# Clustered attention with a Fourier and feed-forward layer: the first sequence's products with the values go three ticks behind the scores, six buffers of transposed probabilities, and the maxima of the later sequences written in place in PSUM

## Chip, cores and metric

The kernel runs on one core of a Trainium2 chip. The metric is the device time of one execution in microseconds (us). Five engines work side by side, each through its own instructions in order: PE (matmuls, with PEld for the loads of stationary operands), DVE (vector), ACT (scalar functions), POOL (a second, slower vector engine) and SP, which here only issues DMAs.

## What is computed

Four sequences of 768 tokens, 8 heads of 64. Queries and keys are each put into one of 16 clusters per head, and a query attends only to keys of its own cluster. The result goes through a two-dimensional Fourier transform with a residual, a layer norm and a feed-forward block.

```
q_assign = argmax(einsum('bhsd,hcd->bhsc', q_n, c_n), axis=-1)      # k_assign likewise
mask = q_assign[:, :, :, None] == k_assign[:, :, None, :]
scores = where(mask, scale * matmul(q, k.T), -1e9)
scores = scores - max(scores, axis=-1, keepdims=True)
attn = exp(scores); attn = attn / (sum(attn, axis=-1, keepdims=True) + 1e-09)
x = matmul(attn, v)                                                # (B, S, H*D)
u = x + real(fft(fft(x, axis=1), axis=2))
un = (u - mean(u)) / sqrt(var(u) + 1e-06)
out = u + relu(un @ w_ch1) @ w_ch2
```

All matmuls are made of fp16 pairs (a high and a low half), so that they come near fp32.

## The kernel before

Heads are worked in pairs: `pr` runs from 0 to 15, four pairs to a sequence. A pair has six tile rows of 128 queries (`st`). In what follows a *tile row* n of the first sequence is 6·pr + st, from 0 to 23. `Overlap.run` writes the whole program out over a clock of its own, in *ticks*: it puts every piece of work into a list under a tick and an order within the tick. In each tick stand, by that order: the scores of one tile row (`att.scores`, order 1), the product with the values of an earlier tile row (`att.attend`, order 3, LAG = 2 ticks after its scores), steps of the next pair's preparation (`att.prep`, `split_v`), and in the first 28 ticks a piece of the weights' preparation (order 6). PE follows this list exactly; on DVE, ACT, POOL and SP the order is made by a scheduler that places instructions when their inputs are due.

A tile row goes through the engines like this, once for each of its two heads (j = 0, 1):

- PE makes the scores in PSUM (L320 and L325, `ps_big`, two buffers).
- DVE takes the row maximum (L339): it multiplies the scores by a negative scale, writes the product somewhere, and keeps the minimum in `rmx`. In the first sequence (`early`) the product goes into one of four strips of X[1] in SBUF and is used; in the later ones it goes into a bf16 tile `ju` that nobody reads.
- ACT takes the exponential (L343 in the first sequence, from the strip; L345 later, from the scores in PSUM) and rounds it to fp16 (L353).
- POOL subtracts that from the exponential to get the low half (L354).
- SP issues one DMA that transposes both halves into a `pt` tile (L356). There are PT = 5 of these.
- In `attend`, PE multiplies `pt` with the values (L374, L375, L376, 36 matmuls to a tile row) into `ps_o`, which has one buffer and takes three tile rows.
- After every third tile row `finish` runs on DVE: L386 and L388 make the reciprocal of the sums, L390 scales `ps_o` into X and so frees it for the next three.

The values come as fp16 pairs in `v16` tiles, four buffers, two of them for one head pair: the split for pair pr + 2 (L199 on ACT, L200 on POOL, L201 on DVE) takes the buffers of pair pr, and so waits for that pair's last `attend`. The weights go through DVE, ACT, POOL and PE too: loaded by SP (L484) into eight raw buffers, their largest taken (L491), split into signs (L519, L520), joined by PE in PSUM (L528), completed by DVE (L532, which frees the raw buffer), and halved (L538, L541, L542, L544).

After a sequence's last tile row `fold` (L660, L661, L641, L642) starts the Fourier work, and from then on each sequence's Fourier and feed-forward matmuls (L713 and others, L858 up, L888 down) fill PE between the next sequence's scores.

Of the kernel before, what the change touches and what calls it, by code (L numbers as in the profile page):

```python
# [15 lines left out]
BF16 = mybir.dt.bfloat16  # L16
# [4 lines left out]
AF = mybir.ActivationFunctionType  # L21
# [4 lines left out]
P = 128  # L26
# [5 lines left out]
SH = S // 2  # L32
# [49 lines left out]
class Attention:  # L82
# [226 lines left out]
    def scores(self, pr, st):  # L309
        nc, sb = self.nc, self.sb  # L310
        assert self.ready >= pr
        (hq, hk), oh, (e, ne) = self.hl[pr], self.oht[pr], self.sc.scores(pr)
        sl = slice(st * P, (st + 1) * P)
        ps = [self.psum().rearrange("p (h x) -> p h x", h=2) for _ in range(2)]
        rows = [slice(D * j, D * (j + 1)) for j in range(2)]
        for hf in range(2):
            hs = slice(hf * SH, (hf + 1) * SH)
            for i, (a, c) in enumerate(((0, 0), (1, 0), (0, 1))):
                for j in range(2):
                    nc.tensor.matmul(out=ps[j][:, hf, 0:SH], lhsT=hq[rows[j], a, sl], rhs=hk[rows[j], c, hs],  # L320
                                     start=(i == 0), stop=False)
        for hf in range(2):
            for j in range(2):
                rz = slice(D * j + 32 * hf, D * j + 32 * hf + 32)
                nc.tensor.matmul(out=ps[j][:, hf, 0:SH].rearrange("p (s x) -> p s x", x=P), lhsT=oh[rz, st % 3 * 2 + st // 3],  # L325
                                 rhs=oh[rz, ST:], start=False, stop=True)
        for j in range(2):

            m = sb.tile([P, 1], F32, name="rmx", tag="rmx", bufs=6)
            early = pr < H // 2  # L330
            if early:

                n = (2 * st + j) % self.RING * S
                p32 = self.X[1].rearrange("p a x -> p (a x)")[:, n:n + S]
            else:
                p32 = sb.tile([P, S], F32, name="p32", tag="p32", bufs=2)
            x = p32.rearrange("p (h x) -> p h x", h=2)
            ju = x if early else sb.tile([P, 2, SH], BF16, name="ju", tag="ju")
            self.mark = nc.vector.tensor_scalar(out=ju, in0=ps[j][:, :, 0:SH], scalar1=ne, scalar2=None, op0=ALU.mult, op1=ALU.min,  # L339
                                    accum_out=m)  # L340
            self.late = m
            if early:
                nc.scalar.activation(p32, p32, AF.Exp, bias=m, scale=-1.0)  # L343
            else:
                nc.scalar.activation(x, ps[j][:, :, 0:SH], AF.Exp, bias=m, scale=e)  # L345
            if early and j:
                ph = sb.tile([P, S], F32, name="p32", tag="p32", bufs=2).bitcast(F16).rearrange("p (a x) -> p a x", a=2)
            else:
                ph = sb.tile([P, 2, S], F16, name="ph", tag="ph", bufs=2)
            if early and j and (st in self.PC):  # L350
                nc.gpsimd.tensor_copy(out=ph[:, 0], in_=p32)
            else:
                nc.scalar.copy(out=ph[:, 0], in_=p32)  # L353
            nc.gpsimd.tensor_tensor(out=ph[:, 1], in0=p32, in1=ph[:, 0], op=ALU.subtract)  # L354
            pt = sb.tile([P, 2 * ST, P], F16, name="pt", tag="pt", bufs=PT)
            nc.sync.dma_start(out=pt, in_=ph.rearrange("p a x -> p (a x)"), transpose=True)  # L356
            self.pt[pr, st, j] = pt
        if st == ST - 1:
            self.hl.pop(pr)
            self.oht.pop(pr)  # L360
# [534 lines left out]
            yield 2.6  # L895


PT = 5


class Overlap:
# [20 lines left out]
    MIX = (1, 0, 0, 0, 1, 0, 0, 1, 1, 0)  # L922
    MIX3 = (0, 0, 0, 0, 0, 0, 0, 1, 1, 1)
    F2 = 1
    PIN, PF, PV = (), 29, 1
    CE, WP, WQ = 0.45, 0, 0

    def layer(self, b, old):
# [52 lines left out]
    def run(self):  # L981
        att, T0, NP = self.att, self.T0, B * H // 2
# [3 lines left out]
        def at(t, order, f, *a):  # L986
            sched.setdefault(max(t, 0), []).append((order, len(sched.get(t, ())), f, a))
# [37 lines left out]
        for pr in range(NP):  # L1025
            t0 = T0 + 6 * pr
            for i, (t, order) in enumerate(self.STEPS if pr else self.STEPS0):
                at(t0 + t, order, (pinned if i in self.PIN and t0 + t >= self.PF else step) if pr else first, att.prep, pr)
            for st in range(ST):
                at(t0 + st, 1, att.scores, pr, st)  # L1030
                at(t0 + st + self.LAG, 3, att.attend, pr, st)
            a, d, e = self.V if pr else self.V0
            at(t0 + a, 7 if pr else 0.1, att.load_v, pr)
            at(t0 + d, 4.5, pin if self.PV and t0 + d >= self.PF else call, att.split_v, 2 * pr)
            at(t0 + e, 4.5, pin if self.PV and t0 + e >= self.PF else call, att.split_v, 2 * pr + 1)
# [81 lines left out]
```

## Time and profile before

| | |
|---|---|
| median of 3 runs | 1053.56 us (1049.64 to 1055.57) |
| the profiled execution | 1049.91 us, its span 1048.1 us |
| PE, DVE, ACT, POOL busy | 87%, 60%, 60%, 56% of the span |

The span is what the trace covers; some 1.8 us lie around it. The shares of busy time are means over stages with different limits: in roughly the first 210 us attention of the first sequence and the weights' preparation run together, later PE's feed-forward work sets the pace. So a stretch of its own has to be read for each.

### The profile page before, as it was taken

How to read it: one execution, taken by the hardware profiler on the slowest of the kernel's cores; microseconds unless marked ns; L12 is line 12 of the kernel's file. 1: busy time of each engine (PE TensorE's matmuls, PEld its weight loads, DVE VectorE, ACT ScalarE, POOL GpSimd, SP SyncE). 2: the span in 40 equal slices, each digit the busy share in tenths (PEclk: the TensorE clock that was granted, in tenths of full speed). 3: DMA queues.
4: the chain of work that ended last, by engine and by line, in shares of the span. 5: the costliest groups of instructions: out<-in, count | busy, mean ns of one | idle time of the engine just before them, and what ended most of it. 6: DMA issues, size and time to landing. Idle time of an engine off the chain costs nothing.

```text
span 1048.1 us, 23542 instructions
## 1 busy us (share of the span) xinstructions
PE 910.8 (87%) x9350; PEld 591.7 (56%) x9362; DVE 627.4 (60%) x1297; ACT 625.3 (60%) x980; POOL 586.9 (56%) x693
## 2 busy tenths in 40 slices
PE   3665565749899999998899999997999999999998
PEld 2333333425575756655666757555757667576674
DVE  8789899767757555668656555667555333631110
ACT  4798889755766665645666746556756543351230
POOL 2364565753975756655856646647847645271230
PEclk9987878769899999999899999998999999999999
DMA  7799998979887776568877767588757562321000
GB/s 272 179 225 245 196 239 166 171 156 153 177 123 153 128 154 121 121 137 161 153 137 142 140 128 132 110 141 170 124 102 133 96 110 43 81 52 31 11 11 21
DMA packets 396239, 140.01 MB, mean 134 GB/s; under 512 B 381784, under 2 KB 381792, under 8 KB 396128
## 3 DMA queue, kind: packets, MB, share of 16 engines
q1 hardware_dynamic: 396128, 138.50, 65.9%
q8 instruction: 73, 1.20, 0.5%
q14 instruction: 38, 0.31, 0.1%
HBM read 42.52 MB, written 6.29 MB: 47 GB/s over the span
## 4 chain that ended last, share of the span: by engine, by line
PE 39%; DVE 6%; DMA 3%; ACT 3%; POOL 2%; issue 2%; SPq 0%; ACTq 0%; DVEq 0%; POOLq 0%
PE ps_f L888 16%; PE ps_f L858 13%; PE ps_big L320 3%; DMA pt<-ph 3%; PE ps_f L713 2%; DVE ju L339 1%; ACT p L345 1%; PE ps_o L374 1%; POOL ph L354 1%; PE ps_o L375 1%; PE ps_o L376 1%; PE ps_big L325 1%; ACT ph L353 1%; DMA scr<-in_k_dram 0%; DVE arena L660 0%
## 5 line engine op out<-in xcount | busy, mean ns | idle before, releaser
L354 POOL TENSOR_TENSOR ph<-p,ph 128x768 f16<-128x768 f32 x144 | 242.9, 1688 | 184.6 <-ACT ph L353 150.1
L858 PE MATMUL ps_f<-arena,w1h 128*128 128x256 f16 x1536 | 271.4, 277 | 19.1 <-ACT arena L866 9.0
L888 PE MATMUL ps_f<-w2h,arena 128*128 128x512 f16 x768 | 238.9, 379 | 0.0
L345 ACT ACTIVATE p<-ps_big,rmx,sce 128x768 f32<-128x768 f32 x144 | 142.1, 988 | 132.9 <-DVE ju L339 127.5
L858 PE MATMUL ps_f<-arena,w1l 128*128 128x256 f16 x768 | 212.4, 277 | 0.0
L339 DVE TENSOR_SCALAR_CACHE_REDUCE ju<-ps_big,sce 128x768 bf16<-128x768 f32 x144 | 146.1, 1014 | 68.2 <-PE ps_big L325 58.2
L888 PEld LDWEIGHTS <-arena 128*128 128x128 f16 x1152 | 108.7, 98 | 126.6 <-issue 5.2
L858 PEld LDWEIGHTS <-w1h 128*128 128x128 f16 x1536 | 152.1, 99 | 36.0 <-issue 14.3
L867 POOL TENSOR_TENSOR arena<-arena 128x256 f16<-128x256 f32 x192 | 128.1, 677 | 77.3 <-ACT arena L866 73.6
L320 PE MATMUL ps_big<-hlk,hlq 64*128 64x384 f16 x1152 | 128.9, 348 | 39.0 <-ACT p L345 23.4
L374 PE MATMUL ps_o<-v,pt 128*128 128x66 f16 x1152 | 124.8, 198 | 43.0 <-DVE X L390 27.5
L888 PE MATMUL ps_f<-w2l,arena 128*128 128x512 f16 x384 | 145.5, 379 | 0.0
L374 PEld LDWEIGHTS <-pt 128*128 128x128 f16 x1152 | 110.2, 100 | 57.7 <-issue 37.1
L353 ACT CAST ph<-p 128x768 f16<-128x768 f32 x144 | 119.6, 832 | 15.0 <-DMA pt<-ph 12.8
L375 PE MATMUL ps_o<-v,pt 128*128 128x64 f16 x1152 | 124.8, 199 | 0.0
L376 PE MATMUL ps_o<-v,pt 128*128 128x66 f16 x1152 | 124.5, 198 | 0.0
L866 ACT ACTIVATE arena<-ps_f,wrel 128x256 f16<-128x256 f32 x192 | 90.1, 472 | 54.8 <-DVE arena L863 54.7
L863 DVE TENSOR_SCALAR arena<-ps_f,wrel 128x256 f32<-128x256 f32 x96 | 46.3, 482 | 124.9 <-PE ps_f L858 66.4
L320 PEld LDWEIGHTS <-hlq 64*128 64x128 f16 x1152 | 55.5, 99 | 101.5 <-issue 72.7
L375 PEld LDWEIGHTS <-pt 128*128 128x128 f16 x1152 | 110.7, 101 | 2.8
L376 PEld LDWEIGHTS <-pt 128*128 128x128 f16 x1152 | 111.1, 103 | 0.0
L858 PEld LDWEIGHTS <-w1l 128*128 128x128 f16 x768 | 76.1, 99 | 20.2 <-issue 10.7
(178 smaller groups left out, 1330.4 us busy)
## 6 DMA issues: line engine op xcount, KB each, us to landing
arena<-in_moe_w_ch_dram SPq DMA_DIRECT2D x32, 512.0 KB, 6.8
scr<-in_q_dram SPq DMA_DIRECT2D x16, 384.0 KB, 2.9
scr<-in_k_dram SPq DMA_DIRECT2D x16, 384.0 KB, 4.5
vst<-in_v_dram SPq DMA_DIRECT2D x16, 384.0 KB, 3.5
out_dram<-arena SPq DMA_DIRECT2D x24, 256.0 KB, 2.3
pt<-ph SPq DMA_TRANSPOSE x168, 3.9
arena<-in_cs_dram SPq DMA_DIRECT2D x12, 192.0 KB, 3.5
arena<-in_ss_dram SPq DMA_DIRECT2D x12, 192.0 KB, 3.5
```

The lines of the kernel that those rows point to most:

```text
L320: nc.tensor.matmul(out=ps[j][:, hf, 0:SH], lhsT=hq[rows[j], a, sl], rhs=hk[rows[j], c, hs], start=(i == 0), stop=False)
L339: self.mark = nc.vector.tensor_scalar(out=ju, in0=ps[j][:, :, 0:SH], scalar1=ne, scalar2=None, op0=ALU.mult, op1=ALU.min, accum_out=m)
L345: nc.scalar.activation(x, ps[j][:, :, 0:SH], AF.Exp, bias=m, scale=e)
L353: nc.scalar.copy(out=ph[:, 0], in_=p32)
L354: nc.gpsimd.tensor_tensor(out=ph[:, 1], in0=p32, in1=ph[:, 0], op=ALU.subtract)
L374: nc.tensor.matmul(out=o[:, at:at + W], lhsT=hi, rhs=v16[:, kt, 0:W], start=(kt == 0), stop=False)
L375: nc.tensor.matmul(out=o[:, at:at + D], lhsT=hi, rhs=v16[:, kt, 66:130], start=False, stop=False)
L376: nc.tensor.matmul(out=o[:, at:at + W], lhsT=lo, rhs=v16[:, kt, 0:W], start=False, stop=(kt == ST - 1))
L858: nc.tensor.matmul(out=ps.rearrange("p (t x) -> p t x", x=P), lhsT=a[:, dc, fs], rhs=c[:, :, dc], start=(i == 0), stop=(i == 11))
L866: nc.scalar.activation(hh[:, f], ps, AF.Relu, scale=rel[:, f:f + 1])
L867: nc.gpsimd.tensor_tensor(out=hl[:, f], in0=r, in1=hh[:, f], op=ALU.subtract)
L888: nc.tensor.matmul(out=ps, lhsT=a[:, f, ts], rhs=c[:, f], start=(i == 0), stop=(i == 47))
```

## The change

Three things. `attend` of tile rows 0 to 21 of the first sequence stands three ticks behind its scores in place of two; rows 22 and 23 stay at two, so that tile rows 21 and 22 are both multiplied in one tick, and the fold comes in the tick where it was. The `pt` tiles are six in place of five. In the later sequences the scaled, negated scores are written over the scores in PSUM, and the exponential reads them there with the scale −1, as it already does from SBUF in the first sequence; the `ju` tile is gone.

```
-        (hq, hk), oh, (e, ne) = self.hl[pr], self.oht[pr], self.sc.scores(pr)
+        (hq, hk), oh, ne = self.hl[pr], self.oht[pr], self.sc.scores(pr)[1]
...
-            ju = x if early else sb.tile([P, 2, SH], BF16, name="ju", tag="ju")
+            ju = x if early else ps[j][:, :, 0:SH]
             self.mark = nc.vector.tensor_scalar(out=ju, in0=ps[j][:, :, 0:SH], scalar1=ne, scalar2=None, op0=ALU.mult, op1=ALU.min,
                                     accum_out=m)
             self.late = m
-            if early:
-                nc.scalar.activation(p32, p32, AF.Exp, bias=m, scale=-1.0)
-            else:
-                nc.scalar.activation(x, ps[j][:, :, 0:SH], AF.Exp, bias=m, scale=e)
+            nc.scalar.activation(x, ju, AF.Exp, bias=m, scale=-1.0)
...
-PT = 5
+PT = 6
...
-    PIN, PF, PV = (), 29, 1
+    PIN, PF, PV, LATE = (), 29, 1, 22
...
-                at(t0 + st + self.LAG, 3, att.attend, pr, st)
+                at(t0 + st + self.LAG + (6 * pr + st < self.LATE), 3, att.attend, pr, st)
```

The numbers of lines below 338 are the same in both kernels; from the exponential on, a line of the kernel before has a number higher by 3 than in the changed one (L390 is L387 there).

**First place: PE, around the scores of tile row 22.** L325 ends the scores (`ps_big`); what follows is an `attend`. `pt_2218` is the transposed first head of tile row 20 in the kernel before.

```order
L325 MATMUL ps_big_2388<-oht_1914 128x384
L325 LDWEIGHTS oht_1914
L325 MATMUL ps_big_2389<-oht_1914 128x384
L374 LDWEIGHTS pt_2218
L374 MATMUL ps_o_2243<-v16_1684,pt_2218 128x66
```

In the changed kernel `pt_2097` is that of tile row 19.

```order
L325 MATMUL ps_big_2352<-oht_1874 128x384
L325 LDWEIGHTS oht_1874
L325 MATMUL ps_big_2353<-oht_1874 128x384
L371 LDWEIGHTS pt_2097
L371 MATMUL ps_o_2308<-v16_1647,pt_2097 128x66
```

So at the same place of PE's queue stands the product of a tile row that is one tick older.

**Second place: DVE, at the end of tile row 17, the sixth `finish`.** The pair of L339 on top is tile row 19 before, and the two single L339 are tile row 20.

```order
253 L339 TENSOR_SCALAR X_64,rmx<-ps_big,sce 128x768 x2
254 L216 TENSOR_REDUCE amx<-scr 128x1
255 L386 TENSOR_SCALAR rs<-ps_o,scp 128x6
256 L532 SCALAR_TENSOR_TENSOR ps_f<-arena,ps_f 128x512
257 L216 TENSOR_REDUCE amx<-scr 128x1
258 L388 RECIPROCAL rs<-rs 128x6
259 L544 SCALAR_TENSOR_TENSOR w2l<-ps_f,wsc,w2h 128x512
260 L201 SCALAR_TENSOR_TENSOR v_2280<-vst,scp,v_2280 128x6x64
261 L339 TENSOR_SCALAR X_64,rmx<-ps_big,sce 128x768
262 L390 TENSOR_TENSOR X_63<-ps_o,rs 128x3x128
```

In the changed kernel the same `finish` (L383, L385, L387) stands with tile row 20, whose two L339 are rows 262 and 266.

```order
259 L216 TENSOR_REDUCE amx<-scr 128x1 x2
260 L541 SCALAR_TENSOR_TENSOR w2l<-ps_f,wsc,w2h 128x512
261 L248 TENSOR_REDUCE amx<-vst 128x1
262 L339 TENSOR_SCALAR X_64,rmx<-ps_big,sce 128x768
263 L383 TENSOR_SCALAR rs<-ps_o,scp 128x6
264 L529 SCALAR_TENSOR_TENSOR ps_f<-arena,ps_f 128x512
265 L385 RECIPROCAL rs<-rs 128x6
266 L339 TENSOR_SCALAR X_64,rmx<-ps_big,sce 128x768
267 L387 TENSOR_TENSOR X_63<-ps_o,rs 128x3x128
```

Before, the freeing L390 stood behind the first maximum of tile row 20, and the next `attend` on PE came right after the scores of that row. Now L387 stands behind the second maximum of row 20, and the next `attend` comes only after the scores of row 21.

**Third place: DVE, at the fold of the first sequence.** L660, L661 and L642 are the fold and its halving; the L339 between them are tile rows of the second sequence.

```order
298 L660 TENSOR_TENSOR arena<-X_63 128x1536
299 L248 TENSOR_REDUCE amx<-vst 128x1
300 L642 SCALAR_TENSOR_TENSOR arena<-arena,vseq 128x768
301 L339 TENSOR_SCALAR ju,rmx<-ps_big,sce 128x768
302 L660 TENSOR_TENSOR arena<-X_63 128x1536
303 L339 TENSOR_SCALAR ju,rmx<-ps_big,sce 128x768
304 L201 SCALAR_TENSOR_TENSOR v_2839<-vst,scp,v_2839 128x6x64
305 L661 TENSOR_TENSOR arena<-arena 128x3x255
306 L642 SCALAR_TENSOR_TENSOR arena<-arena,vseq 128x768
```

The changed kernel has there:

```order
302 L657 TENSOR_TENSOR arena<-X_63 128x1536
303 L248 TENSOR_REDUCE amx<-vst 128x1
304 L339 TENSOR_SCALAR ps_big,rmx<-ps_big,sce 128x2x384 x2
305 L201 SCALAR_TENSOR_TENSOR v_2833<-vst,scp,v_2833 128x6x64
306 L639 SCALAR_TENSOR_TENSOR arena<-arena,vseq 128x768
307 L657 TENSOR_TENSOR arena<-X_63 128x1536
308 L658 TENSOR_TENSOR arena<-arena 128x3x255
309 L639 SCALAR_TENSOR_TENSOR arena<-arena,vseq 128x768
```

Both maxima now stand ahead of the first halving (L639), and nothing of the attention stands between it and the second.

## Rows read from the trace of the kernel before

**Rows 1.** Windows: width, busy us (instructions) by engine, clock, DMA share, GB/s.

```profile
56.00:208.50 152.50, 95.08 (x1176) 58.07 (x1187) 131.56 (x270) 132.61 (x190) 93.34 (x81) 0.80 0.98 207
208.50:262.00 53.50, 37.29 (x429) 22.82 (x431) 39.43 (x72) 29.01 (x43) 25.36 (x21) 0.81 0.85 156
262.00:1048.00 786.00, 749.47 (x7556) 496.54 (x7550) 411.84 (x844) 427.44 (x697) 450.46 (x546) 0.98 0.59 111
```

**Rows 2.** Waits of PE, 56 to 210 us: total us, times, longest.

```profile
PE ps_o L374 <- DVE X L390: 27.5, 6, 5.5
PE ps_o L374 <- DMA pt<-p: 7.4, 7, 2.6
PE ps_o L374 <- DMA pt<-ph: 6.8, 4, 2.2
```

**Rows 3.** Waits of DVE, 56 to 210 us.

```profile
DVE arena L491 <- DMA arena<-in_moe_w_ch_dram: 6.4, 5, 2.0
DVE ps_f L532 <- PE ps_f L528: 3.2, 3, 2.4
DVE ps_f L227 <- PE ps_f L48: 2.1, 2, 2.0
DVE X L339 <- PE ps_big L325: 1.1, 2, 0.6
```

**Rows 4.** Timeline of PE, 176 to 189.5 us: start, length, what, idle before.

```profile
178.49 0.34 PE L325 MATMUL ps_big<-oht 32*128 32x384 bf16 x4
...
183.71 0.19 PE L374 MATMUL ps_o<-v,pt 128*128 128x66 f16 x1 [4.28 <-DVE X L390]
...
187.13 0.24 PE L374 MATMUL ps_o<-v,pt 128*128 128x66 f16 x1 [2.61 <-DMA pt<-p]
...
188.51 1.49 PE L528 MATMUL ps_f<-arena 128*128 128x512 bf16 x3 [0.22 <-issue]
```

**Rows 5.** Timeline of DVE, 180 to 207 us.

```profile
183.01 0.55 DVE L390 TENSOR_TENSOR X<-ps_o,rs 128x384 f32<-128x384 f32 x1
...
189.18 0.70 DVE L532 SCALAR_TENSOR_TENSOR ps_f<-arena,ps_f 128x512 uint32<-128x512 uint32 x1 [2.39 <-PE ps_f L528]
...
206.22 0.57 DVE L227 TENSOR_REDUCE ps_f<-ps_f 128x3 f32<-128x384 f32 x1 [1.95 <-PE ps_f L48]
```

**Rows 6.** Windows, instructions that touch `ps_o`: width, PE and DVE busy us (instructions).

```profile
56.00:208.50 152.50, 34.70 (x723) 5.35 (x14) 0.80 0.98 207
```

**Rows 7.** Windows, instructions of L263: width, PE and PEld busy us (instructions).

```profile
56.00:208.50 152.50, 2.49 (x36) 0.86 (x36) 0.80 0.98 207
```

**Rows 8.** Timeline of DVE at the fold, 218.5 to 238.5 us.

```profile
227.35 1.41 DVE L642 SCALAR_TENSOR_TENSOR arena<-arena,vseq 128x768 f16<-128x768 f32 x1 [3.23 <-ACT arena L641]
228.69 1.00 DVE L339 TENSOR_SCALAR_CACHE_REDUCE ju<-ps_big,sce 128x768 bf16<-128x768 f32 x1
...
235.64 1.31 DVE L642 SCALAR_TENSOR_TENSOR arena<-arena,vseq 128x768 f16<-128x768 f32 x1 [1.00 <-ACT arena L641]
```

**Rows 9.** Groups on DVE by form, 56 to 210 us: busy us, mean ns, idle before.

```profile
L339 DVE TENSOR_SCALAR_CACHE_REDUCE X<-ps_big,sce 128x768 f32<-128x768 f32 x40 | 39.1, 1010 | 1.6 <-PE ps_big L325 1.1 <-POOL ac L281 0.5
L532 DVE SCALAR_TENSOR_TENSOR ps_f<-arena,ps_f 128x512 uint32<-128x512 uint32 x27 | 18.2, 688 | 3.3 <-PE ps_f L528 3.2
L60 DVE TENSOR_SCALAR winv<-arena 128x4 int32<-128x4 int32 x4 | 6.2, 1547 | 0.1
L544 DVE SCALAR_TENSOR_TENSOR w2l<-ps_f,wsc,w2h 128x512 f16<-128x512 f32 x8 | 5.9, 737 | 0.0
L60 DVE TENSOR_SCALAR winv<-arena 128x1 int32<-128x1 int32 x3 | 0.5, 150 | 0.0
```

**Rows 10.** Groups on DVE by line, 262 to 1000 us.

```profile
L339 DVE TENSOR_SCALAR_CACHE_REDUCE ju<-ps_big,sce 128x768 bf16<-128x768 f32 x132 | 133.9, 1015 | 66.5 <-PE ps_big L325 57.0 <-ACT arena L866 2.0 <-DVE ju L339 0.9
```

**Rows 11.** Waits of PE, 262 to 1048 us.

```profile
PE ps_big L320 <- ACT p L345: 8.7, 7, 3.0
```

**Rows 12.** Waits of POOL, 56 to 210 us.

```profile
POOL v L200 <- PE ps_o L376: 16.5, 4, 7.1
```

## Prediction

> **What bounds the kernel now.** I read the windows first, because one share of busy time over the whole span hides two different kernels. In the last 786 us PE is busy for 749.47 of 786.00, 95%, at a clock of 0.98 [rows 1]: there only PE's own work counts. The change takes nothing from that work: the same matmuls, in a slightly different order. In the stretch from 56 to 208.5 us, which is most of the first sequence, PE is busy for 62%, but DVE for 131.56 and ACT for 132.61 of 152.50, 86% and 87%, and the DMA engines stand at 0.98 [rows 1]. There DVE and ACT hand one tile row to each other and are both nearly full. So the end of that stretch is set by the work of these two and by the time in which they wait, some 20 us on either. From 208.5 to 262 us nobody is full: the fold has a chain of its own. Whatever the change brings must come out of these two stretches and is then carried unchanged to the end, since PE's work behind them is fixed.
>
> Then the waits. PE waits most where the change aims: 27.5 us in 6 products for L390 to free `ps_o`, and 7.4 + 6.8 us for the transposed probabilities [rows 2]. That is 41.7 us, but it is time of an engine with 38% to spare. What counts is how much of it comes back to DVE. DVE's own list is much shorter: 6.4 us for weights from DMA, 3.2 us for the joined weights (L528 on PE), 2.1 us for L48 on PE, 1.1 us for scores [rows 3]. Only 6.4 us of it is PE's lateness.
>
> One place shows how a wait of PE becomes one of DVE. PE ends tile row 20's scores at 178.49 + 0.34 = 178.83 us. Its next product needs `ps_o` and starts at 183.71, right after L390 at 183.01 on DVE, which stood in DVE's queue behind a maximum. The product's second head then waits 2.61 us for its transposition, and only behind it comes L528 at 188.51 [rows 4]. DVE, which needs that join for L532, has been idle for 2.39 us when it starts at 189.18 [rows 5]. The 1.95 us ahead of L227 at 206.22 [rows 5] come in the same way, through L48 behind a product.
>
> **The change, part by part.** The sum is made against the profiled execution, 1049.91 us; the median of the runs shown, 1053.56 us, is 3.65 us above it.
>
> *Three ticks in place of two.* A tick is 152.5 us over 20 tile rows (40 maxima [rows 9]), 7.6 us. The transposition gets one tick more to land; the waits for it were 2.6 us at most [rows 2], so they go. The wait for L390 goes too, by the order of the queues and not by the delay itself: the `finish` moves one tile row down on DVE, yet in seven of its eight cases (the last is unchanged) it now stands before the maxima of the scores behind which the next product sits on PE (the second place shown above: L387 is behind row 20's maxima, the product behind row 21's scores). Then joins and L48 follow products that do not wait, and the 3.2 + 2.1 us of L532 and L227 [rows 3] should go. I leave 0.3 of it and take **−5 us**. Lower bound: also the 1.1 us of L339, −6.4. Upper bound: 0, if DVE then waits for ACT at the same instants.
>
> *Weights from DMA.* The scheduler has laid DVE's other work anew around the moved `finish`. A raw buffer is freed by L532 and its refill first read by L491, eight pieces of weight later. Adding up mean durations along DVE's queue between the two, I find five of 24 such distances under 3 us in the order before, and two in the new one; a refill can't land in that time, and the trace has five waits there, 6.4 us together [rows 3]. I take half of it back: **−3 us** (0 to −6.4).
>
> *New waits.* A `finish` now stands with the tile row whose tick also has the 12 matmuls of L263 ahead of the product. That happens three times (ends of tile rows 5, 11 and 17). PE needs 2.49 / 3 = 0.83 us for them [rows 7] and 34.70 / 20 = 1.73 us for a product (723 matmuls at 36 each) [rows 6], so 2.56 us after the scores. DVE reaches L383 after one maximum (1.01 us [rows 9]) and at most two short instructions more, so it idles up to 2.56 − 1.01 = 1.55 us, three times 4.65 us. The two cases with other work in between get less: **+2 us** (0 to 7.7, three times the whole 2.56, if ACT's split of the values, held by the same product, delays the next exponential too).
>
> *Six buffers.* With three ticks all six are needed in each tick: both transpositions of a tile row wait for the product in the same tick. They come late anyway, since maximum, exponential, rounding and subtraction lie between scores and DMA. From the second sequence on the distance stays two, and PE never waited for `pt` there, so the sixth buffer is worth **0**. If the cover goes, it is the slower rival below.
>
> *The fold.* Before, the first halving L642 stands ahead of tile row 26's maxima and waits 3.23 us for ACT, and the maximum behind it starts only at 228.69 [rows 8]. Now both maxima come first, and nothing of the attention lies between first and second halving (third place above). That frees the next scores by some 3 us and the second halving, at 235.64 before, by about 2. PE then has to wait for the fold's transpositions, so I count **−1.5 us** (0 to −4.2, both waits of the rows together, 3.23 + 1.00).
>
> *Maxima in place.* No row shows this instruction writing PSUM. The nearest pair is L532, which works in place in PSUM, 688 ns for 512 elements, against L544, which reads PSUM and writes SBUF, 737 ns [rows 9]: writing PSUM is 49 ns cheaper there, 74 ns for 768 elements. The bf16 output costs as much as the fp32 one (1015 [rows 10] and 1010 ns [rows 9]). I take the maximum as unchanged, with ±0.1 us as bounds. On the path it lies only where PE waited for the exponential: 7 waits, 8.7 us [rows 11]; 7 × 0.1 us is below 1 us. **0**, cover: PE's own work.
>
> Sum: −5 − 3 + 2 − 1.5 = −7.5 us. 1049.91 − 7.5 = 1042.4 us in a profile, and 3.65 us more, **1046 us**, as a median.
>
> **A rule that speaks against it.** L60 on four columns takes 1547 ns each of four times, on one column 150 ns [rows 9]. So 5.6 us of DVE's "busy" time is four instructions being held up. The Trainium skill (SBUF — State Buffer, "SBUF: two separate sides") says why: VectorE in a two-port mode and GpSimd share a port pair under an exclusive lock, and the loser blocks for the other's whole instruction. The trace's row is what such a lock would leave; which instruction of POOL held it, the row doesn't say. By it, work freed of one wait can run into another: L58 and L59, eight more instructions of that width, may be caught like L60. By the rows that would be up to 8 × 1.4 = 11 us, and the sum would be +3.5 us. That is the third rival.
>
> **The rivals.**
>
> 1. *PE's waits were free.* For it: of 41.7 us on PE only 6.4 reach DVE, ACT is as full as DVE, and the DMA engines stand at 0.98. When DVE no longer waits for PE, it would wait for ACT or a DMA at the same place. Against: DVE's largest single waits (2.39, 1.95) have nothing else behind them. Then only the fold's part stays: −1.5, 1052 us.
>
> 2. *Slower: buffers come free one tick later.* The `v16` buffers of a pair are freed by its last product, now one tick later, while the split that wants them stays in its tick. POOL's small memset L200 waited 16.5 us in 4 cases for that product [rows 12], with the low halves L354 queued behind it; and all transpositions wait for a product of the same tick, with weights' loads queued behind them on SP. In the new POOL queue the first memset stands between the low halves of tile row 6 and waits for a product behind the scores of row 8, two ticks on. The strips in X[1] are four, so the maximum four heads later waits for that low half. If each of three such places costs half a tick, 3.8 us, that is +11.4 on the gains, 1046 + 11.4 = 1057 us. It decides when POOL is held more than about 5 us beyond what it is held now. Against: POOL is busy for 61% of that stretch only (93.34 of 152.50 [rows 1]) and was held up to 7.1 us already [rows 12] without DVE waiting for L354.
>
> 3. *The port.* As above, 1046 + 11 = 1057 at most; half of it, 1051 to 1052, is what I would expect of it.
>
> **How the numbers follow.** My forecast has 0.60, with a range of its own of 1037 to 1052; rival 1 0.20, rival 3 0.06, rival 2 0.14. A measurement of this kernel can tell about 0.5%, 5.3 us, from no change: below 1048.3 is faster, above 1058.8 slower. Of the forecast's 0.60 some 0.05 lies within the bound: faster 0.55. Within: 0.05 + 0.20 + 0.06 and a little of rival 2, 0.33. Slower: 0.12. The lower end of the range is the sum of the lower bounds, −6.4 − 6.4 − 4.2 = −17 us, 1036 us and a half; the upper end is rival 2 as worked out, 1057 us, and a bit: 1058. Outside of it are a stronger rival 2 and gains that nobody sees in these rows, together less than 2 in 10.
>
> **What would show it.** Right: in the new profile PE's wait for L387 in the first sequence falls from 27.5 us to under 8, and that for `pt` to near 0; DVE's waits for L528 and L48 vanish; the first maximum of the second sequence, which ends the stretch at 208.5 us now, comes some 6 us earlier; the windows from 262 us on are as long as now. Wrong: DVE's busy share from 56 us on stays at 86% although PE no longer waits (rival 1); POOL's wait at L200 exceeds 25 us, or SP's wait for `ps_o` shows up at L356's successor L353 (rival 2); L58 to L60 exceed 1 us more often (rival 3); the maximum in PSUM takes over 1.1 us or PE waits longer for exponentials.

## The result, and the profile after

The changed kernel takes 1056.57 us (median of 20 runs, 1051.45 to 1060.93), the kernel before 1051.53 us (median of 20, 1047.82 to 1056.61). The ratio is 1.0041, 95% interval 1.0026 to 1.0056: slower by 4 us by the ratio and by 5 us by the medians, where 7.5 us less were forecast. The difference is under 0.5%, but the interval excludes no change, and the sign is the other one.

The profiled execution of the changed kernel happened to be its fastest, 1051.45 us with a span of 1049.7 us. So its trace shows less of the loss than the median does, and I took a second one (below).

From the exponential on, a line of the changed kernel has a number lower by 3 than in the kernel before. First the windows of the changed kernel, cut at its own first maximum of the second sequence, with columns as in [rows 1]:

```profile
56.00:203.50 147.50, 96.59 (x1222) 58.86 (x1231) 132.68 (x272) 132.23 (x190) 93.65 (x81) 0.84 1.02 215
203.50:262.00 58.50, 43.44 (x485) 28.35 (x483) 46.23 (x88) 30.20 (x46) 31.79 (x27) 0.80 0.81 150
262.00:1049.00 787.00, 747.44 (x7487) 493.37 (x7486) 403.60 (x828) 411.60 (x692) 444.71 (x539) 0.98 0.58 111
```

The first sequence ends at 203.5 us in place of 208.5: 5 us earlier, near the 6 that were forecast. DVE works 90% of that stretch (132.68 of 147.50) where it was 86%. Then its waits of PE and of DVE from 56 to 210 us (total us, times, longest), to be read against [rows 2, 3]:

```profile
PE ps_big L320 <- DVE X L339: 23.3, 22, 2.9
PE ps_f L525 <- DVE w2l L541: 5.1, 1, 5.1
PE ps_o L371 <- DMA pt<-p: 4.8, 3, 3.2
...
PE ps_f L525 <- DVE w1l L541: 3.8, 1, 3.8
...
PE ps_o L371 <- DMA pt<-ph: 2.6, 1, 2.6
```

```profile
DVE arena L488 <- DMA arena<-in_moe_w_ch_dram: 8.1, 5, 2.6
DVE amx L216 <- DMA scr<-in_q_dram: 4.0, 2, 3.2
...
DVE ps_f L529 <- PE ps_f L525: 0.8, 1, 0.8
```

PE's 27.5 us for L390 are gone, and so are DVE's waits for L48 and for scores; that for the joined weights fell from 3.2 to 0.8. What PE waits for now is DVE itself (L541, and L339 for twice as long as before), which costs DVE nothing. In the kernel before, in the same stretch:

```profile
PE ps_big L320 <- DVE X L339: 11.0, 12, 3.7
```

So the aim was reached, and still the end is later. To see where the time goes I compare one instruction in both traces: PE's first score matmul (L320) of each tile row. Tile rows are counted on through the four sequences here, 0 to 95. PE's program is the same in both kernels from tile row 24 on, so a difference in these start times is a delay and nothing else. Worked out from the timelines of PE (changed minus before, us; the second line is the second trace of the same kernel):

```
tile row          25    28    32    36    42    53    59    76    84    95
changed         -5.1  -5.9  -7.1  -3.9  -1.8  +0.3  +0.7  +0.0  +1.8  +1.4
changed again   -2.4  -1.0  +0.1  +2.0  +4.1  +6.2  +6.6  +6.3  +7.5  +7.1
```

The two traces differ by 2.7 us at tile row 25, by 7.2 at 32 and by some 6 from 36 on. From tile row 28 to 95 the changed kernel loses 7.3 us in the one and 8.1 in the other, in steps (32 to 36, 39 to 42, 49 to 53, 76 to 84). "Windows from 262 us on are as long as now" was wrong. Between the steps PE is full in both kernels and they run in parallel (rows 42 to 49: 56.0 us each).

TensorE's granted clock is not what makes the 7.3 us. Behind tile row 28 it falls to the lower of its two levels (1.2 in place of 2.4 GHz) once in each later sequence, at 270, 498 and 724 us in the kernel before; ahead of the fall at 498 us PE had been busy for 14.71 of 18 us. Between the first scores of rows 28 and 95 the lower level lasts 23.9 us in the trace before and 23.9 in the changed one, worked out from the clock records of the traces. In the second trace it is 33.9 us, so part of its 8.1 us may be the clock's.

### The profile page after: what moved, and what is told of

Read it like the earlier page. It is cut to its first block, busy times and chain, and to the rows that moved or that the text cites. A ratio compares the mean times of both kernels' runs of the same rounds, so it can differ in the third digit from the quotient of the medians.

```text
span 1049.7 us, 23525 instructions
## 1 busy us (share of the span) xinstructions
PE 916.4 (87%) x9350; PEld 593.8 (57%) x9362; DVE 626.8 (60%) x1297; ACT 610.5 (58%) x980; POOL 588.4 (56%) x693
## 4 chain that ended last, share of the span: by engine, by line
PE 41%; DVE 21%; DMA 11%; ACT 10%; issue 8%; POOL 8%; SPq 0%; ACTq 0%; POOLq 0%; DVEq 0%
PE ps_f L885 18%; PE ps_f L855 12%; DMA pt<-ph 5%; DVE ps_big L339 4%; PE ps_big L320 4%; POOL ph L351 3%; ACT ph L350 3%; DVE X L339 2%; DMA vst<-in_v_dram 2%; PE ps_f L710 2%; DMA arena<-in_moe_w_ch_dram 1%; ACT p L342 1%; PE ps_o L371 1%; DVE arena L488 1%; POOL arena L864 1%
## 5 line engine op out<-in xcount | busy, mean ns | idle before, releaser
L351 POOL TENSOR_TENSOR ph<-p,ph 128x768 f16<-128x768 f32 x144 | 241.5, 1684 | 182.5 <-ACT ph L350 151.8
L855 PE MATMUL ps_f<-arena,w1h 128*128 128x256 f16 x1536 | 270.4, 276 | 21.0 <-ACT arena L863 11.4
L855 PE MATMUL ps_f<-arena,w1l 128*128 128x256 f16 x768 | 211.5, 275 | 0.0
L342 ACT ACTIVATE p<-ps_big,rmx 128x768 f32<-128x768 f32 x144 | 128.7, 899 | 126.9 <-DVE ps_big L339 111.8
L320 PE MATMUL ps_big<-hlk,hlq 64*128 64x384 f16 x1152 | 133.8, 354 | 47.7 <-DVE X L339 26.7
L864 POOL TENSOR_TENSOR arena<-arena 128x256 f16<-128x256 f32 x192 | 129.1, 682 | 74.9 <-ACT arena L863 71.2
L855 PEld LDWEIGHTS <-w1h 128*128 128x128 f16 x1536 | 151.6, 99 | 33.6 <-issue 10.0
L339 DVE TENSOR_SCALAR_CACHE_REDUCE ps_big<-ps_big,sce 128x768 f32<-128x768 f32 x144 | 141.4, 1020 | 46.2 <-PE ps_big L325 44.0
L863 ACT ACTIVATE arena<-ps_f,wrel 128x256 f16<-128x256 f32 x192 | 90.6, 474 | 69.9 <-DVE arena L860 68.2
L320 PEld LDWEIGHTS <-hlq 64*128 64x128 f16 x1152 | 57.6, 99 | 111.2 <-issue 73.8
L855 PEld LDWEIGHTS <-w1l 128*128 128x128 f16 x768 | 75.8, 99 | 24.9 <-issue 15.7
```

The lines of the kernel that those rows point to most:

```text
L342: nc.scalar.activation(x, ju, AF.Exp, bias=m, scale=-1.0)
L855: nc.tensor.matmul(out=ps.rearrange("p (t x) -> p t x", x=P), lhsT=a[:, dc, fs], rhs=c[:, :, dc], start=(i == 0), stop=(i == 11))
L863: nc.scalar.activation(hh[:, f], ps, AF.Relu, scale=rel[:, f:f + 1])
L864: nc.gpsimd.tensor_tensor(out=hl[:, f], in0=r, in1=hh[:, f], op=ALU.subtract)
```

## The experiments

All ratios are to the kernel before, run on the same chip; "drift" is the table above for the kernel in question. No kernel leaves out work. First each part alone.

**Three ticks alone**, with `ju` in SBUF and five buffers:

```
+    PIN, PF, PV, LATE = (), 29, 1, 22
...
+                at(t0 + st + self.LAG + (6 * pr + st < self.LATE), 3, att.attend, pr, st)
```

> The kernel before with the products of the first sequence three ticks behind, still five buffers of transposed probabilities and the maxima's throw-away values in SBUF. Theory A (the three ticks gain what was forecast, and the loss comes from the maxima in PSUM): some 5 to 7 us below the kernel before, about 1045, and the first maximum of the second sequence near 203 us. Theory B (the gain of the first sequence is given back later whatever else is done, since PE's work behind it is fixed in another way than I took it): the second sequence starts 5 us earlier, but the end stays within 2 us of the kernel before. Theory C (the three ticks themselves cost more later than they give): 4 us or more above it. With five buffers a transposition waits one tick longer for its buffer; if that matters, PE's waits for pt come back, up to the 14 us of before, and the second sequence starts at 206 to 208 us.

Measured: 1057.40 us, 1.0054 (1.0030 to 1.0077). Drift +2.3 at tile row 25, +4.7 at 28, +7.1 at 36, +8.4 at 95: nothing was gained in the first sequence, and 2.4 us went between 32 and 36. PE's waits for `pt` did not come back (0.4 us), but DVE's for weights from DMA rose to 10.7 us from 6.4 [rows 3]. From row 42 on this kernel is parallel to the one before (+7.7 to +8.4). Theory A's "lag alone gains" does not hold for five buffers. The granted clock was also lower in this trace, 0.59 from 31 to 56 us and 0.76 from 56 to 200, against 1.00 and 0.81 before; how much of the early loss is the clock's stays open.

**Maxima in place alone** (two ticks, five buffers):

```
-PT = 6
+PT = 5
...
-    PIN, PF, PV, LATE = (), 29, 1, 22
+    PIN, PF, PV, LATE = (), 29, 1, 0
```

> The kernel before with the maxima in place in PSUM alone; products two ticks behind, five buffers. Theory A: 5 to 10 us above the kernel before, with the loss in the tile rows 32 to 42, 50 to 57 and 74 to 82, and nothing gained before tile row 24 (first maximum of the second sequence at 208 to 209 us). Theory B: at most 5 us above the kernel before, for B needs a loss too, but it would lie with the earlier start of the second sequence and so not here: within 2 us. Theory C: the same as the kernel before.

Measured: 1057.44 us, 1.0042 (1.0026 to 1.0058). Drift +1.6 at tile row 25, +5.2 at 36, +6.8 at 42, +8.2 at 53, +9.6 at 84, +9.2 at 95. The later loss of the changed kernel is here too, in the same places, without any three ticks. Theory B falls: nothing had been gained that could be given back.

**The changed kernel with five buffers** (`PT = 5`):

> The changed kernel with five buffers in place of six. If the sixth buffer is worth something with three ticks, PE's waits for pt in the first sequence rise from 7.2 us to 15 or more and the time rises by 2 to 5 us over the changed kernel, to 1059 or more; if it is worth nothing there (my 0), the time is that of the changed kernel within 2 us, 1055 to 1058.

Measured: 1058.09 us, 1.0059 (1.0036 to 1.0081). Drift +3.1 at tile row 25, where the changed kernel has -5.1 and -2.4; behind row 28 it loses 5.9 us like the others. `pt` is not what PE waits for (1.2 us in the first sequence); DVE waits 9.2 us for weights from DMA. By the medians the sixth buffer gives 1.5 us with overlapping intervals, and with another number of buffers the scheduler also made another order; what it is worth with three ticks stays open.

**The changed kernel with two ticks throughout** (`LATE` 0):

> The changed kernel without the three ticks: two ticks throughout, six buffers, maxima in PSUM. Every queue's order is that of the maxima in PSUM alone, so only the sixth buffer tells the two apart: equal within 1 us if my 0 holds. Against the changed kernel it shows what the three ticks are worth in its company: by theory A some 5 us slower than it (1060 to 1062), by theory B the same (1056 to 1057), by theory C faster (about 1052).

Measured: 1055.36 us, 1.0035 (1.0017 to 1.0053). Drift -0.8 at tile row 25, -0.4 at 36, +3.0 at 53, +3.7 at 95. Every queue has the order of the in-place kernel with five buffers, so the sixth buffer alone is worth 0 to 2 us there (the intervals overlap).

So the kernels with maxima in place lose 5.6 to 8.1 us behind tile row 28. The instruction itself can hardly be the reason: its mean is 1020 ns where it was 1015 [rows 10], and the read of its accumulator 141 ns where it was 83 (rows in the last section), on an engine that is busy for half of that time (403.60 of 787.00 us). But the order of DVE, ACT, POOL and SP is made by a scheduler, and it makes another order for the changed instruction, for the whole program. The next runs take the two apart: they impose a given order on these four queues, by edges that say only "issue behind" and wait for nothing.

```
+def queue_orders(nc, tc):
...
+    for e, text in ORDERS.items():
...
+        for a, b in zip(row, row[1:]):
+            tc.add_manual_dep(b, a.name, free, reason="queue_orders")
```

**Maxima in place and six buffers, in the order of the kernel before:**

> Maxima in place and six buffers, products two ticks behind, as in the run of that name before, but with the instructions of DVE, ACT, POOL and SP in exactly the order that they have in the kernel before. Theory A1 (the maxima in PSUM cost nothing themselves; the loss of 5.7 us between tile rows 32 and 95 is that of the new order that the scheduler made of their changed costs): the drift against the kernel before is flat from tile row 32 on, within 1 us, and the time is within 2 us of it, 1050 to 1054. Theory A2 (the instruction, or the buffers of PSUM that it holds, costs): the same 5 to 6 us are lost as with the new order, 1055 to 1058.

Measured: 1050.82 us, 0.9991 (0.9974 to 1.0009). Drift 0.0 at tile row 28, -0.1 at 42, -0.7 at 95. The 5.6 us are gone; same instructions, same buffers as the run before.

**The kernel before, in the order made for maxima in place:**

> The kernel before, every instruction as it was, with DVE, ACT, POOL and SP in the order that the scheduler made for the maxima in place (two ticks). Theory A1: it loses 5 to 6 us between tile rows 32 and 95 in the same places as that kernel (rows 32 to 42, 50, 80 to 83), 1056 to 1058. Theory A2: within 2 us of the kernel before.

Measured: 1060.23 us, 1.0089 (1.0065 to 1.0113). Drift -1.3 at tile row 28, +4.6 at 42, +8.6 at 59, +10.9 at 95. No instruction changed, and the loss is there, larger than forecast. These two runs settle it: the order costs, not the maxima; and the edges cost nothing that shows, for the run before has them too. In the new order the changed instructions even do better than the old ones (1.0035 against 1.0089); why was not tried.

**The changed kernel, its own order up to tile row 28, that of the kernel before behind it:**

> The changed kernel, whole, with its own order of the queues up to tile row 28 and behind it the order of the kernel before. Theory A1: the gain of 5 to 6 us at tile row 28 is carried to the end, and the time is 5 us below the kernel before, 1045 to 1048. Theory B (what the first sequence gains is given back whatever the order): 1050 to 1054. Theory A2: 1055 or more.

Measured: 1047.19 us, 0.9960 (0.9942 to 0.9977). Drift -1.8 at tile row 25, -3.5 at 28, -3.7 at 36, -2.6 at 53, -5.1 at 95: the gain of the first sequence is carried to the end, as the prediction said, once the old order stands there. Against the same kernel with two ticks throughout (0.9991), three ticks are worth 0.3%, some 3 us (the intervals just overlap).

**The changed kernel again:**

> The changed kernel once more, for a second trace, since its profiled run was the fastest of its runs. If its trace was typical, the second sequence starts again 5 us before that of the kernel before (203 to 205 us) and 7 us are lost again behind it; if not, at 206 us or later, with the same loss behind it.

Measured: one run, 1057.43 us; its drift stands above. The second sequence starts at 206.2 us, at the edge of what was called untypical; the loss behind tile row 28 is 8.1 us.

What differs in that order? One thing stands out on ACT. In 65 of the 72 tile rows from 24 on, the kernel before rounds the first head's probabilities (L353) between the two exponentials. The order made for maxima in place puts both exponentials first and the rounding behind them in 65 of 72. Here is the place where PE first loses: ACT around the exponentials of tile row 32, in the changed kernel in its own order,

```profile
282.37 0.47 ACT L862 ACTIVATE arena<-ps_f,wrel 128x256 f32<-128x256 f32 x1 [2.21 <-POOL arena L864]
282.74 0.47 ACT L863 ACTIVATE arena<-ps_f,wrel 128x256 f16<-128x256 f32 x1
283.09 1.69 ACT L342 ACTIVATE p<-ps_big,rmx 128x768 f32<-128x768 f32 x2
284.66 0.84 ACT L350 CAST ph<-p 128x768 f16<-128x768 f32 x1
285.38 0.61 ACT L266 ACTIVATE ac<-ps_f,cinv 128x384 f32<-128x384 f32 x1
```

and the same instructions with the old order behind tile row 28:

```profile
282.44 0.47 ACT L862 ACTIVATE arena<-ps_f,wrel 128x256 f32<-128x256 f32 x1
282.80 0.48 ACT L863 ACTIVATE arena<-ps_f,wrel 128x256 f16<-128x256 f32 x1
283.76 0.90 ACT L342 ACTIVATE p<-ps_big,rmx 128x768 f32<-128x768 f32 x1 [0.49 <-DVE ps_big L339]
284.67 0.58 ACT L266 ACTIVATE ac<-ps_f,cinv 128x384 f32<-128x384 f32 x1
285.15 0.82 ACT L350 CAST ph<-p 128x768 f16<-128x768 f32 x1
```

L266 copies the similarities to the clusters out of PSUM, and PE's next feed-forward matmul needs that buffer. In the new order it stands behind two exponentials and a rounding (2.3 us after the first exponential's start), in the old one behind one exponential (0.9 us). On PE, in the changed kernel:

```profile
286.04 0.27 PE L855 MATMUL ps_f<-arena,w1h 128*128 128x256 f16 x1 [1.31 <-ACT ac L266]
```

With the old order that wait isn't in the list. ACT is late ahead of the exponentials already: it stands idle for 2.21 us before L862, a ReLU into a buffer that POOL's L864 has to free. In the changed kernel POOL works a subtraction of the probabilities (L351) and one of the layer norm (L825) ahead of that L864,

```profile
278.64 1.64 POOL L351 TENSOR_TENSOR ph<-p,ph 128x768 f16<-128x768 f32 x1
280.23 1.15 POOL L825 TENSOR_TENSOR arena<-arena 128x512 f16<-128x512 f32 x1
281.35 0.99 POOL L864 TENSOR_TENSOR arena<-arena 128x256 f16<-128x256 f32 x1
```

and with the old order it does L864 ahead of L825, and ACT does not wait:

```profile
281.41 0.67 POOL L864 TENSOR_TENSOR arena<-arena 128x256 f16<-128x256 f32 x1
282.05 0.19 POOL L837 TENSOR_SCALAR rt<-rt 128x2 f32<-128x2 f32 x1
282.21 2.27 POOL L825 TENSOR_TENSOR arena<-arena 128x512 f16<-128x512 f32 x2
```

Another way is through `ph`, of which there are two: a later rounding makes POOL's subtraction and the transposition late, the next rounding waits for that transposition, and the ReLUs behind it on ACT (L862, L863) wait too, which PE needs. Waits from 279 to 1043 us (us, times, longest): the changed kernel,

```profile
ACT ph L350 <- DMA pt<-ph: 19.2, 24, 2.2
...
ACT arena L862 <- POOL arena L864: 16.1, 11, 2.2
...
PE ps_f L855 <- ACT arena L863: 11.4, 15, 1.8
...
PE ps_f L855 <- DVE ac L279: 3.9, 3, 1.8
PE ps_f L710 <- DMA arena<-arena: 2.9, 2, 2.1
PE ps_f L855 <- ACT ac L266: 1.6, 2, 1.3
```

and the same kernel with the old order behind tile row 28:

```profile
ACT ph L350 <- DMA pt<-ph: 12.2, 10, 2.1
ACT arena L862 <- POOL arena L864: 8.7, 9, 1.6
...
PE ps_f L855 <- ACT arena L863: 8.8, 11, 1.2
PE ps_f L855 <- DMA arena<-arena: 5.3, 2, 3.0
...
PE ps_f L855 <- DVE ac L279: 1.8, 3, 1.4
```

All of PE's waits in this stretch come to 32.1 us in the changed kernel, 26.1 with the old order behind tile row 28, and 27.9 in the kernel before. Not all of them shrink with the old order: the one for a DMA (L855) is 5.3 us there and 1.0 in the changed kernel.

Roundings wait for a transposition 24 to 27 times in four traces with the new order (changed, changed again, two ticks, and the kernel before in that order), and 10 to 13 times in three with the old one. The next runs test whether that pair on ACT is the whole of it.

**The changed kernel's own order, but the rounding ahead of the second exponential in 55 tile rows from 28 on:**

> The changed kernel in its own order everywhere, but for one pair on ACT: in 55 of the tile rows from 28 on, where the kernel before rounds the first head's probabilities (L353) between its two exponentials and the changed kernel does it behind both, the rounding goes ahead of the second exponential again. Theory A1a (that pair is the whole of the loss, since a later rounding makes the subtraction, the transposition and the next rounding on that buffer late, with ReLUs queued behind it): the drift behind tile row 28 is within 1.5 us, and the time 1047 to 1050, as with the whole old order. Theory A1b (the loss is many places on several queues, SP's order of the fold's transpositions among them): at least half of it stays, 1053 to 1057.

Measured: 1054.76 us, 1.0019 (1.0005 to 1.0033). By the medians some 2 us come back, with overlapping intervals; the trace, of the slowest of the 12 runs, shows no gain (drift +0.9 at tile row 28, +8.4 at 95). L266 still stands behind both exponentials, and PE waits 1.5 us for it in rows 32 to 36; ahead of them ACT still waits 2.0 us for POOL at L862, since POOL's order is as it was. Theory A1b.

**The kernel before, with that pair turned round in the same 55 rows:**

> The kernel before in its own order everywhere, but for the same pair in the same 55 tile rows: the first head's rounding behind the second exponential. Theory A1a: it loses 5 to 8 us behind tile row 28, 1057 to 1060. Theory A1b: at most 3 us, 1051 to 1055.

Measured: 1070.04 us, 1.0156 (1.0132 to 1.0179). Drift -0.4 at tile row 28, +4.4 at 42, +10.1 at 59, +16.9 at 84. Neither theory: the one pair costs some 17 us in an order that is otherwise made for the rounding in the middle. So the pair and the rest of the queues belong together; its price depends on them. Part of the 17 us may be the clock's: between the first scores of tile rows 28 and 95 the lower level lasts 41.0 us in this trace, and 23.9 in the one before.

**The changed kernel with one line of its source, everything else left to the scheduler:**

```
+            with contextlib.nullcontext() if early or not j else self.tc.issue_after(cast.ins):
+                nc.scalar.activation(x, ju, AF.Exp, bias=m, scale=-1.0)
...
-                nc.scalar.copy(out=ph[:, 0], in_=p32)
+                cast = nc.scalar.copy(out=ph[:, 0], in_=p32)
```

> The changed kernel with one line that holds the second head's exponential behind the first head's rounding from the second sequence on; the scheduler lays everything else itself. Theory A1a: about 1047 to 1050, below the kernel before. Theory A1b: within 2 us of the changed kernel, 1055 to 1058, or anywhere between if the scheduler makes yet another order.

Measured: 1046.74 us, 0.9939 (0.9920 to 0.9959), the fastest of all by its median and equal, within the intervals, to the run with the old order. Drift -1.2 at tile row 28, -0.1 at 42, -1.2 at 59, -3.7 at 84, -3.9 at 95. With the rounding held in the middle, the scheduler lays the rest nearer to the old order too: in its queue L266 stands ahead of the second head's rounding for every head pair from the seventh on, while the changed kernel's own order has it behind both roundings for seven of these ten.

But at tile row 32, the first of these ten, L266 stands here as in the run with the one pair turned: behind exponential, rounding and exponential. There PE waited 1.5 us for it; here it does not wait, and ACT does not wait for POOL ahead of it either. Waits of ACT from 279 to 1043 us, first in the run with the one pair turned, then here (lines from L342 on are higher by 1 here):

```profile
ACT ph L350 <- DMA pt<-ph: 17.5, 18, 3.0
ACT arena L862 <- POOL arena L864: 14.4, 11, 2.0
```

```profile
ACT ph L351 <- DMA pt<-ph: 12.3, 17, 2.3
...
ACT arena L863 <- POOL arena L865: 7.1, 8, 1.3
```

The roundings wait about as often in this fastest kernel as in that slow one. ACT's wait for POOL tells them apart. It is 14.3 to 16.1 us in the seven traces with the new order of POOL, and 6.1 to 8.8 us in the six with the old order or with this line. The turned pair in the old order, slowest of all, has 10.5 us, so this is not the whole of it either; no run turned POOL's order alone.

**The control: the kernel before with the same line:**

> The kernel before with the line that holds the second head's exponential behind the first head's rounding from the second sequence on (it does so in 65 of 72 tile rows without it): a control for the changed kernel with that line. If the 5 us by which that one beat the kernel before are the change's own (three ticks, six buffers, maxima in place), this one is within 2 us of the kernel before or above it, 1050 to 1056; if the line itself gives them, it is near 1047.

Measured: 1051.42 us, 0.9991 (0.9972 to 1.0010). The line gives the kernel before nothing; the 0.6% come from the change with the line. The control's trace is of a run of 1055.11 us and loses 5.8 us between tile rows 28 and 95 (drift -0.7, then +1.1 at 53, +5.5 at 80, +5.1 at 95), with the clock at its lower level for 37.5 us there, although the median is that of the kernel before. So a drift behind tile row 28 in one trace is not yet a loss; what carries the argument above is the medians.

## Why the prediction was wrong

The step that failed is this one: "Whatever the change brings must come out of these two stretches and is then carried unchanged to the end, since PE's work behind them is fixed." PE's work is fixed: from the first scores of tile row 42 to those of 49 it takes 56.0 us in all these traces but two, which have 56.2 and 56.4. But 5% of the stretch from 262 us on were waits [rows 1], and the waits are set by the order of the other queues. The prediction read the new order at the fold, and wrote off the in-place maxima with "0, cover: PE's own work" from the instruction's duration. The queues behind the fold were not read, ACT's above all, where exponentials and roundings changed places in 55 tile rows from 28 on. With the old order there, the changed kernel is 0.40% faster (4.2 us, and 6.4 with the one line of source, where 7.5 were forecast); with its own, 0.41% slower. The difference, 0.81% or 8.5 us, is what the re-made order costs.

Point by point:

- **-5, PE's waits that come back to DVE.** The mechanism is shown as far as DVE's waits go: L532's wait for L528 is 0.8 us in place of 3.2, those for L48 and for scores are gone [rows 3]. PE's wait for `pt` fell from 14.2 us [rows 2] to 7.4, not to near 0. The gain at tile row 25 is 5.1, 2.4, 1.8 and 0.0 us in four traces with that order up to tile row 28 (changed, changed again, old order behind it, the pair turned behind it). What makes them differ stays open; the last has the lowest clock of the four from 31 to 56 us, 0.52.
- **-3, weights from DMA.** Wrong sign: 8.1, 8.0, 9.3 and 8.5 us in those four traces, where it was 6.4 [rows 3]. Mean durations along a queue did not tell when a refill lands. By the first of them the term is off by 4.7 us; the four gains lack 0.9 to 6.0 us against the forecast of 6 for the first sequence (the +2, which did not come either, makes up for part of it).
- **+2, new waits of the `finish`.** Not there: no trace of the four lists a wait of L383 on DVE.
- **-1.5, the fold.** From tile row 25 to 28: -0.8, +1.4, -1.7 and +0.9 us in the four traces. The runs can't tell it from 0.
- **0, six buffers.** With two ticks 0 to 2 us; with three ticks open.
- **0, maxima in place.** Right for the instruction, as the in-place kernel in the old order shows (0.9991); wrong for what it sets off.
- **Range and rivals.** 1056.57 us lies inside the range, 1036 to 1058, and near rival 2's 1057, but for another reason: that is luck. Rival 2 wanted POOL's wait at L200 above 25 us; it fell from 16.5 [rows 12] to 1.9. Rival 1 wanted DVE to stay at 86%; it is 90%. No rival had a re-made order.
- **Rival 3, the port.** L60 on four columns takes 164 ns now where it took 1547 [rows 9]. But the prediction's price for L58 and L59 left out that L59 was caught in the kernel before already:

```profile
L59 DVE TENSOR_SCALAR arena<-arena 128x4 int32<-128x4 int32 x4 | 4.6, 1143 | 0.1
L58 DVE TENSOR_SCALAR arena<-arena 128x4 int32<-128x4 int32 x4 | 0.8, 211 | 0.0
```

In the changed kernel L58 is caught in L60's place, and L59 less:

```profile
L58 DVE TENSOR_SCALAR arena<-arena 128x4 int32<-128x4 int32 x4 | 3.3, 830 | 0.0
...
L59 DVE TENSOR_SCALAR arena<-arena 128x4 int32<-128x4 int32 x4 | 3.1, 785 | 0.1
...
L60 DVE TENSOR_SCALAR winv<-arena 128x4 int32<-128x4 int32 x4 | 0.7, 164 | 0.1
```

These rows are groups on DVE from 56 to 210 us (busy us, mean ns). The three groups have 7.1 us together, where they had 11.6. That is hardly a gain for DVE, since eight instructions of another short group (L293, 128x96) take 853 ns on average where they took 411, 3.5 us more. The Trainium skill (SBUF — State Buffer, "SBUF: two separate sides") has the loser of the port pair blocked for the other's whole instruction; that the stall moves between short neighbours agrees with it, but no run here shows which instruction of POOL held them.

What stays open: which of the order's differences costs how much (L266 behind the roundings, the rounding itself, POOL's order ahead of L864, SP's order of the fold's transpositions, for which PE waits 2.9 us at L710). The runs that turned one pair alone show that they don't add up singly. Also open is why the scheduler chose so: it follows from the changed maxima and exponentials (with three ticks alone, ACT keeps the rounding in the middle in 63 of the 72 tile rows), but which of the two moves it was not tried.

## What to carry to other kernels

Where a scheduler lays the queues, an edit of one instruction is also an edit of every queue to the program's end: compare the order of all engines through to the end, and read first the in-order engine on which another engine's release can slip behind something that waits. To tell a bad edit from a bad order, impose the old order on the new instructions and the new order on the old ones; two runs settle it. And when a good edit comes with a bad order, one constraint at the place that matters (here: round before the second exponential) can bring the rest back.

## What the runs showed of the hardware

The exponential that reads PSUM became cheaper, which I had not counted on. Groups on ACT and DVE from 262 to 1000 us (busy us, mean ns), first the kernel before, then the changed one:

```profile
L345 ACT ACTIVATE p<-ps_big,rmx,sce 128x768 f32<-128x768 f32 x132 | 130.3, 988 | 117.3 <-DVE ju L339 114.3 <-POOL ph L354 3.1
...
L339 DVE DVE_READ_ACCUMULATOR ju<-ps_big,sce 128x1 f32 x132 | 11.0, 83 | 0.0
```

```profile
L342 ACT ACTIVATE p<-ps_big,rmx 128x768 f32<-128x768 f32 x132 | 118.1, 900 | 109.5 <-DVE ps_big L339 96.1 <-POOL ph L351 3.7 <-POOL rpow L838 3.3
...
L339 DVE TENSOR_SCALAR_CACHE_REDUCE ps_big<-ps_big,sce 128x768 f32<-128x768 f32 x130 | 127.8, 1020 | 45.7 <-PE ps_big L325 43.4 <-ACT ph L350 2.2
L339 DVE DVE_READ_ACCUMULATOR ps_big<-ps_big,sce 128x1 f32 x130 | 18.3, 141 | 0.0
```

It takes 900 ns for 988. Two things changed for it, the constant scale in place of the column `sce`, and scores that DVE has written over; which of them does it was not tried. The Trainium skill (ScalarE: Activation LUTs, "What ACT_TABLE_LOAD costs") has each per-partition operand of an activation add some 93 ns over a constant; the 88 ns here agree with that. The read of the accumulator behind a maximum that writes PSUM takes 141 ns for 83. Also, one program's first 28 tile rows varied by 4.9 us between two executions, and the control's trace lost 5.8 us behind them with an unchanged median: a single trace prices a stretch to no better than some 5 us.
